# Two mixtures in 9 blocks of 512 columns instead of 10 of 464, with one load buffer for q and k and new planner settings

## The chip, the cores and the metric
The kernel runs on one core of a Trainium2 chip. The metric is the time of one execution on the device in microseconds (us), of which several runs are taken; a profile is one more execution, recorded by the hardware. TensorE does the matrix products (PE in the profile, PEld for its weight loads), VectorE (DVE), ScalarE (ACT) and GpSimd (POOL) do elementwise work, and SyncE (SP) issues all transfers, in one queue and in order.

## The reference
Three layers follow one another, all in f32, with batch 8, sequence 576 and model width 512. First an attention with 8 heads of 64 that keeps only scores close to the row's maximum:

```python
scores = scale * np.matmul(q, k.transpose(0, 1, 3, 2))
thresh = np.max(scores, axis=-1, keepdims=True) - tau
scores = np.where(scores >= thresh, scores, -1000000000.0)
attn = softmax(scores); x = np.matmul(attn, v)        # heads side by side: (8, 576, 512)
```

Then a first mixture, in which each position is mixed with the one before it in the same sequence (`mu_k * x + (1 - mu_k) * x_prev`, and the same with `mu_r`), and a second, whose gate is a convolution of 5 taps along the sequence:

```python
v = np.maximum(xk @ w_k, 0.0) ** 2 @ w_v              # 512 -> 1024 -> 512
x = sigmoid(xr @ w_r) * v
gate = sigmoid(sum(conv_w[j] * x shifted by 4 - j))   # zero before the start of a sequence
out = (gate * (x @ w_val)) @ w_out
```

## The kernel before
Activations lie transposed: 128 partitions of the model width (four of them, KD = 4) by positions. For accuracy every matmul operand of the mixtures is split in a rounded high part and a rest ("h" and "l", "hi" and "lo" in the names), and each product is the sum of three matmuls: high by high, high weights by the rest, and the weights' rest by high. `mm3` (line 719) writes this order, and all mixture matmuls are issued in line 728. The weights w_k and w_v come as 64-bit floats and are turned into the two parts on the chip by `split_weight` (line 354: two ScalarE, one VectorE and two GpSimd operations and the two that make the parts, in pieces of 512 columns; w_v's pieces go through one staging buffer, w_k's through three).

The attention goes over 32 pairs of heads, each in 9 chunks (`chunk`, line 477): QK matmuls (line 501), minimum on VectorE (526), exp on ScalarE (539), mask on VectorE (548), norm on GpSimd (561), a copy of the probabilities from p to pr by a transfer (615), transposes (585), and the AV matmuls at chunks 3 and 8 (651, 654). `prep` (418) loads q and k of one head of the next pair into a buffer "raw" (428), casts q (435) and k (431) on ScalarE, makes k's rest kl on VectorE (439) and q's rest on GpSimd (445), and frees the buffer. There are two such buffers (RAWS = 2, line 281), and the loads are planned at chunk 1 and chunk 4.

The first mixture (`moe1`, 833) works on blocks of TW = 464 columns. Each sequence is preceded by 4 columns of zeros (PAD = 4), so 8 sequences are 8 x 580 = 4640 columns, 10 blocks; the zeros let a block run over the end of a sequence without regard to it. `mix_k` (814) makes the mixed input of a block by `shift_mix` (762), in one operation per sequence that the block touches; then come 96 matmuls with w_k, a relu, a square and a split, and 96 with w_v. The results v go to memory. The second mixture (`block2`, 943) loads x and v of each block, mixes x (lines 775 and 785, over the whole block at once), makes r (48 matmuls), a sigmoid, y = gate x v (994), the convolution (tap 0 on ScalarE, 1033, taps 1 to 4 on VectorE, 1036, on a tile that has 4 columns of the block before ahead of it), then val and out (48 matmuls each), and stores.

The order of all this on each engine is written out by a planner (`Plan.order`, line 81) before the program is built: each operation has an engine, a duration, a key (lower goes first) and tokens for its buffers, and a list schedule turns them into one fixed order for each engine. At run time each engine keeps to that order and waits by semaphores. The keys hang on constants in lines 201 to 232: one unit is a batch of attention, softmax work of chunk g has the key g/36 - EARLY, and so on.

Of the kernel before, what the change touches and what calls it, by code (L numbers as in the profile page):

```python
# [40 lines left out]


# [13 lines left out]
class Plan:  # L56
# [24 lines left out]
    def order(self, hop):  # L81
# [22 lines left out]
        while events:  # L104
# [11 lines left out]
            for e in ENGINES:  # L116
                while busy[e] <= now and ready[e]:
# [73 lines left out]
                    for x in pick.after:  # L191
                        x.ready = max(x.ready, end + pick.lat + (SAME.get(e, 0.0) if x.eng == e else hop))
# [35 lines left out]
SWITCH = 200.0  # L228
GANG = 2.6953
# [8 lines left out]
def body(ctx, tc, qka, qkb, vp, w_k, w_v, w_r, w_val, w_out, conv_w, par, out):  # L238
# [14 lines left out]
    v_d = [dram.tile([128, KD, TW], F32, name=f"v_d{n}") for n in range(NBK)]  # L253
# [27 lines left out]
    XBUFS, RAWS = 6, 2  # L281
# [40 lines left out]
    SQ, K_LO = {"act": 497, "pool": 1160}, {"dve": 555, "pool": 1160}  # L322
# [396 lines left out]
    def mm3(ps, w, a, m, kcs):  # L719
# [13 lines left out]
    def product(w, a, m, K, parts, prio, rel=(), cap=("mm",), each=()):  # L733
# [7 lines left out]
        for run, uses, first, end in mm3(ps, w, a, m, list(range(K))):  # L741
# [10 lines left out]
            o = op("pe", 210 * len(uses), go, deps, prio, acq=cap + (BANKS,) if first else (),  # L752
# [9 lines left out]
    def shift_mix(w, src, prio, tiles, pool_, tag, toks, eng, opened=None, psum=False):  # L762
# [4 lines left out]
        for c in range(KD):  # L767
# [3 lines left out]
            for x, (get, at, k, deps) in enumerate(got):  # L771
                def prev(c=c, f=f, get=get, at=at, k=k, x=x):
                    if psum:
                        f["p"] = bank(f["op"])[:, 0:TW]
                        nc.scalar.activation(out=f["p"], in_=get()[:, 0:k], func=AF.Copy, scale=omu[w][:, c:c + 1])
                        return
                    if x == 0:
                        f["f"] = f["p"] = pool_().tile([128, TW], F32, name="xf", tag="xf", bufs=2)
# [3 lines left out]
                def mix(c=c, f=f, get=get, at=at, k=k):  # L782
                    if psum:
                        f["f"] = pool_().tile([128, TW], F32, name="xf", tag="xf", bufs=2)
# [4 lines left out]
                if psum:  # L789
                    o = f["op"] = chain("mix", op("act", 497, prev, first + [last.get("mix")], prio, acq=(BANKS, "xp")))  # L790
                    ps.append(chain("mixd", op("dve", 130 + 1.04 * k, mix, (o, last.get("mixd")), prio, acq=toks[:1],
                                               rel=(o, "xp"))))
                    continue
# [12 lines left out]
            h = chain(tag, op("act", 497, hi, ps + [last.get(tag), opened], prio, acq=toks[1](c)))  # L806
            l = f["lo"] = op(eng, 0, lo, (h,), prio, rel=toks[:1], port=True)
# [6 lines left out]
    def mix_k(n, prio):  # L814
        def src(c):
            return [(lambda b=b, s0=s0, k=k: x_t[b, c][:, s0:s0 + k + 1], at, k, (x_done[b, c],))
                    for b, s0, k, at in pieces(n)]

        def tiles(c):
            return [m1_p.tile([128, TW], F32R, name="xk" + x, tag="xk" + x, bufs=XKBUFS) for x in "hl"]  # L820
# [334 lines left out]
```

## Time and profile before

| | |
|---|---|
| time, median of 3 runs | 1237.56 us (1234.44 to 1240.56) |
| the profiled execution | 1239.84 us, span from the first to the last instruction 1238.1 us |
| busy in the span | PE 1200.3 us (97%), PEld 1013.0, DVE 865.2 (70%), ACT 868.8 (70%), POOL 723.3 (58%) |
| mixture matmuls (line 728) | 47% of the chain of waits that ended last |
| granted TensorE clock, mean | 0.996 |

Busy times of PE overlap, since its matmuls are pipelined and their ends are modelled; how fast they follow each other is read from their starts. Times in the rows are us from the start of the span, "ns" where it says mean.

### The profile page before, as it was taken

The numbers are of one execution on the slowest core, as the hardware profiler recorded it, in microseconds if no ns is written. First come the engines' busy times: TensorE is split into PE (matmuls) and PEld (weight loads), VectorE is DVE, ScalarE is ACT, GpSimd is POOL, SyncE is SP. The second block draws the span as 40 slices with busy tenths as digits, with TensorE's granted clock in tenths as the row PEclk, the third lists the DMA queues.
The fourth block names the chain that finished last, engine by engine and source line by source line (L and its number), as shares of the span: only waits on it lengthen the run. The fifth ranks groups of instructions, "written<-read, shape, count | busy, mean of one in ns | idle before, by whom it ended". The sixth has DMA issues, their size and how long they took to land.

```text
span 1238.1 us, 21148 instructions
## 1 busy us (share of the span) xinstructions
PE 1200.3 (97%) x7134; PEld 1013.0 (82%) x7134; DVE 865.2 (70%) x1894; ACT 868.8 (70%) x1673; POOL 723.3 (58%) x979
## 2 busy tenths in 40 slices
PE   6889999999999999999999999999999999999998
PEld 4667788877888888787878788888888888888887
DVE  7999887787788898787778687751315985555440
ACT  7899877876887886785776785763545775555442
POOL 5798866875776887466666564540306764444321
PEclk9899999999999999999999999999999999999999
DMA  6366545567456666455645455225106332221011
GB/s 241 108 198 243 204 183 208 206 205 278 175 198 245 233 209 224 166 216 188 221 157 219 156 188 191 114 114 199 62 16 238 109 123 92 93 93 62 31 46 62
DMA packets 71501, 201.62 MB, mean 163 GB/s; under 512 B 10848, under 2 KB 28384, under 8 KB 70624
## 3 DMA queue, kind: packets, MB, share of 16 engines
q1 hardware_dynamic: 71392, 200.26, 45.5%
q8 instruction: 57, 0.93, 0.3%
q14 instruction: 52, 0.43, 0.1%
HBM read 91.18 MB, written 34.73 MB: 102 GB/s over the span
## 4 chain that ended last, share of the span: by engine, by line
PE 67%; DMA 4%; ACT 3%; DVE 1%; issue 1%; POOL 1%; ACTq 0%; DVEq 0%; POOLq 0%; SPq 0%
PE g L728 47%; PE s L501 8%; PE g L651 6%; PE g L585 4%; DMA pr<-p 4%; PE g L654 2%; ACT p L539 1%; DVE p L548 1%; ACT pt L598 0%; POOL p L561 0%; DVE sm L526 0%; DVE kl L439 0%; POOL qkh L445 0%; ACT qkh L431 0%; POOL sm L529 0%
## 5 line engine op out<-in xcount | busy, mean ns | idle before, releaser
L548 DVE SCALAR_TENSOR_TENSOR p<-s,sm,p 128x576 f32<-128x576 f32 x288 | 229.3, 812 | 58.6 <-ACT p L539 43.5
L526 DVE TENSOR_REDUCE sm<-s 128x1 f32<-128x576 f32 x288 | 212.6, 750 | 71.9 <-PE s L501 65.7
L539 ACT ACTIVATE p<-s,sm 128x576 f32<-128x576 f32 x288 | 210.0, 750 | 59.7 <-DVE sm L526 31.1
L561 POOL TENSOR_SCALAR p<-p,sm 128x576 f32<-128x576 f32 x234 | 189.1, 814 | 107.3 <-DVE sm L558 96.8
L501 PE MATMUL s<-qkh 128*128 128x288 f32 x620 | 196.6, 333 | 10.5 <-DVE p L548 8.0
L501 PE MATMUL s<-kl,qkh 128*128 128x288 f32 x620 | 173.6, 295 | 0.0
L598 ACT ACTIVATE pt<-g 128x512 f32<-128x512 f32 x256 | 145.0, 606 | 22.5 <-PE g L585 21.3
L529 POOL TENSOR_SCALAR sm<-sm,gs 128x1 f32<-128x1 f32 x288 | 110.4, 386 | 79.9 <-DVE sm L526 63.7
L651 PE MATMUL g<-pt,v 128*64 128x320 f32 (+1 forms) x1024 | 140.4, 417 | 0.7 <-ACT ptl L609 0.4
L501 PEld LDWEIGHTS s<-qkh 128*128 128x128 f32 x620 | 116.9, 188 | 22.8 <-issue 7.3
L585 PE MATMUL g<-ident_r,pr 128*128 128x128 f32 (+1 forms) x1148 | 121.6, 242 | 6.4 <-DMA pr<-p 4.0
L585 PEld LDWEIGHTS g<-ident_r,pr 128*128 128x128 f32 (+1 forms) x1148 | 116.0, 140 | 14.2 <-ACT p L539 3.5
L728 PE MATMUL g<-kh,w_v_hi 128*128 128x464 f32 x320 | 122.6, 383 | 0.0
L728 PE MATMUL g<-xkh,w_k_hi 128*128 128x464 f32 x320 | 121.2, 379 | 0.0
L501 PEld LDWEIGHTS s<-kl,qkh 128*128 128x128 f32 x620 | 117.2, 189 | 4.6
L728 PE MATMUL g<-xkh,w_k_lo 128*128 128x464 f32 x320 | 119.2, 373 | 0.0
L728 PE MATMUL g<-kh,w_v_lo 128*128 128x464 f32 x320 | 119.1, 372 | 0.0
L651 PEld LDWEIGHTS g<-pt,v 128*64 128x64 f32 x1024 | 68.7, 138 | 56.2 <-issue 11.5
L445 POOL TENSOR_TENSOR qkh<-raw,qkh 64x576 fp32r<-64x576 f32 x62 | 91.9, 1482 | 24.9 <-ACT qkh L435 18.7
L1036 DVE SCALAR_TENSOR_TENSOR g<-y,cw_t,g 128x464 f32<-128x464 f32 x160 | 103.9, 697 | 1.3 <-ACT g L1033 0.6
L1068 POOL TENSOR_TENSOR gvl<-gate,gvh 128x464 fp32r<-128x464 f32 x40 | 48.2, 1206 | 71.8 <-ACT gvh L1065 67.6
L1003 POOL TENSOR_TENSOR yl<-y,yh 128x464 fp32r<-128x464 f32 x40 | 50.6, 1272 | 63.2 <-ACT yh L1000 53.9
(113 smaller groups left out, 2678.3 us busy)
## 6 DMA issues: line engine op xcount, KB each, us to landing
pr<-p SPq DMA_DIRECT2D x112, 576.0 KB, 3.5
raw<-in_qkb SPq DMA_DIRECT2D x31, 640.0 KB, 4.6
raw<-in_qka SPq DMA_DIRECT2D x31, 608.0 KB, 3.8
v<-in_vp SPq DMA_DIRECT2D x32, 320.0 KB, 3.0
x_d<-x SPq DMA_DIRECT2D x32, 290.0 KB, 4.4
v_d<-vo SPq DMA_DIRECT2D x40, 232.0 KB, 2.0
vt<-v_d SPq DMA_DIRECT2D x10, 928.0 KB, 4.6
pr<-p SPq DMA_DIRECT2D x28, 288.0 KB, 2.7
```

The source lines that it names most:

```text
L445: nc.gpsimd.tensor_tensor(out=t["hi"][lo_rows, qs], in0=t["raw"][lo_rows, qs], in1=t["hi"][lo_rows, qs].bitcast(F32), op=ALU.subtract)
L501: nc.tensor.matmul(s_t[g][:, hh, 0:NT], lhsT=q, rhs=k, start=(i == 0), stop=(i == len(terms) - 1))
L526: nc.vector.tensor_reduce(out=sm[:, 0:1], in_=s_t[g][:, :, 0:NT], op=ALU.min, axis=AX.XY)
L529: nc.gpsimd.tensor_scalar(out=sm_t[g][:, 1:2], in0=sm_t[g][:, 0:1], scalar1=tau_t, scalar2=1.0, op0=ALU.add, op1=ALU.mult)
L539: nc.scalar.activation(out=view(), in_=s_t[g][:, :, 0:NT], func=AF.Exp, bias=sm_t[g][:, 0:1], scale=-1.0)
L548: nc.vector.scalar_tensor_tensor(out=view(), in0=s_t[g][:, :, 0:NT], scalar=sm[:, 1:2], in1=view(), op0=ALU.is_le, op1=ALU.mult, accum_out=to)
L561: nc.gpsimd.tensor_scalar(out=view(), in0=view(), scalar1=sm_t[g][:, 3:4], scalar2=1.0, op0=ALU.mult, op1=ALU.mult)
L585: nc.tensor.transpose(o_.bitcast(F32R), in_=i_.bitcast(F32R), identity=ident_r)
L598: nc.scalar.activation(out=pt[:, head, :, q0:q0 + 128], in_=ps.rearrange("p (k q) -> p k q", k=4), func=AF.Copy)
L651: nc.tensor.matmul(acc[h * 64:h * 64 + 64, 0:n], lhsT=v[:, kc * 128 + h * 64:kc * 128 + h * 64 + 64], rhs=pt[:, h, kc, 0:n], start=(kc == ...
L728: nc.tensor.matmul(ps()[:, 0:TW], lhsT=W[w][wt][:, kc, m * 128:(m + 1) * 128].bitcast(F32R), rhs=a(at, kc), start=(i == 0 and x == 0), sto ...
L1036: nc.vector.scalar_tensor_tensor(out=f["ps"], in0=t["y"][:, c, k:k + TW], scalar=cw[:, c, k:k + 1], in1=f["ps"], op0=ALU.mult, op1=ALU.add)
```

## The change
Both mixtures go over 9 blocks of MW = 512 columns of the 8 x 576 = 4608 columns, without padding. A generator `spans` gives the pieces of a block that lie in one sequence; 7 of the 9 blocks have two, the first and the last have one. The first mixture had one operation per piece already in its mix; now the second mixture's x mix has one ScalarE and one VectorE operation per piece too, and each convolution tap on VectorE one per piece, cut short at a sequence's start. The tap that ScalarE does is now the one without shift, which doesn't wait for the 4 columns of the block before. x is loaded with one more column per piece. The buffers for v in the second mixture go from 2 to 1, those of its output from 3 to 2, and the load buffers of q and k from 2 to 1 (RAWS). The planner gets durations for the new width, 471 ns more latency after each transfer (DMA_MARGIN), 0.2% on the durations of three engines (MARGIN), and new values for nearly all keys. The cut diff:

```diff
+MW = 512
+NM = B * S // MW
+def spans(at, end):
+    start = at
+    while at < end:
+        b, s = divmod(at, S)
+        k = min(S - s, end - at)
+        yield b, s + PAD, k, at - start
+        at += k
 ...
+                    if e in ("dve", "act", "pool"):
+                        pick.dur *= MARGIN
 ...
-                        x.ready = max(x.ready, end + pick.lat + (SAME.get(e, 0.0) if x.eng == e else hop))
+                        x.ready = max(x.ready, end + pick.lat + (DMA_MARGIN if e == "dma" else 0.0) + (SAME.get(e, 0.0) if x.eng == e else hop))
 ...
-EARLY, QK_EARLY, T_LATE, EV_EARLY, AV_LATE = 12.6663, 0.7557, -0.5953, 253.4919, 0.4078
+EARLY, QK_EARLY, T_LATE, EV_EARLY, AV_LATE = 13.0706, 0.7631, -0.6414, 57.4969, 0.5687
-MOE_LAG = 0.4575
-MOE_STEP = 0.816
+MOE_LAG = 0.6961
+MOE_STEP = 0.8287
-MIX_EARLY, SIDE_EARLY = 0.978, 0.0233
-W_KEY, W_STEP = -3.2244, 709.0823
-V_KEY, V_STEP = 3.7242, -1.2805
+MIX_EARLY, SIDE_EARLY = -4.6463, 0.4707
+W_KEY, W_STEP = -3.234, 266.006
+V_KEY, V_STEP = 18.3214, -0.5937
-HOP = 240.0
-VAL_LAG, OUT_LAG = 1.7452, 2.9004
-LATE2, LOAD2, MIX2, CONV_LAG, THR_EARLY = -13.6721, -99.7979, 7.3987, 1044.9074, 358.4791
-MIX_AT = 28.3782
-OUT_FETCH = 281.3772
-PORT_TOL, PORT_SLACK = 1851.8404, 0.196
+HOP, DMA_MARGIN, MARGIN = 257.8425, 470.7487, 1.002
+VAL_LAG, OUT_LAG = 1.5662, 2.9644
+LATE2, LOAD2, MIX2, CONV_LAG, THR_EARLY = 6.1443, -14.9596, -12.7571, 18129.9782, 561.2799
+MIX_AT = 431.1075
+OUT_FETCH = 278.4628
+PORT_TOL, PORT_SLACK = 1556.9636, 1.1934
-GANG = 2.6953
+GANG = 6.4091
 ...
-    XBUFS, RAWS = 6, 2
+    XBUFS, RAWS = 6, 1
 ...
-                    nc.tensor.matmul(ps()[:, 0:TW], lhsT=W[w][wt][:, kc, m * 128:(m + 1) * 128].bitcast(F32R),
+                    nc.tensor.matmul(ps()[:, 0:tw], lhsT=W[w][wt][:, kc, m * 128:(m + 1) * 128].bitcast(F32R),
 ...
-    for n in range(NBK):
-        moe1(n, 1 + MOE_LAG + n * MOE_STEP)
+    for n in range(NM):
+        moe1(n, 1 + MOE_LAG + n * MOE_STEP * MW / TW)
 ...
-                  vt=2, y=2, yh=2, gv=2, o=3, cv=CVB, xp=2)
+                  vt=1, y=2, yh=2, gv=2, o=2, cv=CVB, xp=2)
 ...
             def tap(c=c, k=1, f=f):
-                nc.vector.scalar_tensor_tensor(out=f["ps"], in0=t["y"][:, c, k:k + TW],
-                                               scalar=cw[:, c, k:k + 1], in1=f["ps"],
-                                               op0=ALU.mult, op1=ALU.add)
+                for b, s0, w, at in parts_of:
+                    x = at + (4 - k if s0 == PAD else 0)
+                    nc.vector.scalar_tensor_tensor(out=f["ps"][:, x:at + w], in0=t["y"][:, c, x + k:at + w + k],
+                                                   scalar=cw[:, c, k:k + 1], in1=f["ps"][:, x:at + w],
+                                                   op0=ALU.mult, op1=ALU.add)
```

## Rows read from the trace of the kernel before
**Rows 1.** Busy time by windows: us; PE, PEld, DVE, ACT, POOL; clock, DMA, GB/s
```profile
0.00:50.00 50.00, 38.16 (x215) 25.45 (x215) 39.52 (x77) 38.56 (x74) 31.60 (x53) 0.93 0.61 209
50.00:100.00 50.00, 42.47 (x292) 31.42 (x291) 47.62 (x98) 48.90 (x99) 45.12 (x67) 1.00 0.43 142
100.00:150.00 50.00, 47.20 (x323) 39.10 (x322) 44.25 (x90) 43.84 (x88) 44.16 (x60) 1.00 0.66 234
...
950.00:1000.00 50.00, 50.00 (x241) 44.86 (x240) 47.70 (x77) 40.05 (x77) 38.60 (x34) 1.00 0.41 142
```
**Rows 2.** The chain that ended last, in order of time: start us, us, what
```profile
307.77 1.88 PE g L651 x16
...
353.34 2.30 PE g L651 x16
...
846.74 98.16 PE g L728 x467
944.91 288.94 PE g L728 x1381
```
**Rows 3.** TensorE's groups: names, shape, count, busy us, mean ns, idle before
```profile
L728 PE MATMUL g<-xkh,w_k_hi 128*128 128x464 f32 x320 | 121.2, 379 | 0.0
...
L728 PE MATMUL g<-xrh,w_r_hi 128*128 128x464 f32 x160 | 59.7, 373 | 0.0
```
**Rows 4.** TensorE's timeline: start us, us, what; QK steps, then mixture steps
```profile
310.24 0.30 PE L501 MATMUL s<-kl,qkh 128*128 128x288 f32 x1
...
311.57 0.29 PE L501 MATMUL s<-kl,qkh 128*128 128x288 f32 x1
...
1211.16 0.37 PE L728 MATMUL g<-yh,w_val_hi 128*128 128x464 f32 x1
...
1216.16 0.37 PE L728 MATMUL g<-yh,w_val_hi 128*128 128x464 f32 x1
```
**Rows 5.** VectorE's groups: taps, kl, two sizes of the first mix
```profile
L1036 DVE SCALAR_TENSOR_TENSOR g<-y,cw_t,g 128x464 f32<-128x464 f32 x160 | 103.9, 697 | 1.3 <-ACT g L1033 0.6
...
L439 DVE SCALAR_TENSOR_TENSOR kl<-raw,gs,qkh 128x640 fp32r<-128x640 f32 x31 | 44.2, 1426 | 0.6 <-ACT qkh L431 0.5
...
L785 DVE SCALAR_TENSOR_TENSOR xf<-x,par_t,xf 128x464 f32<-128x464 f32 x16 | 13.7, 858 | 1.3 <-POOL xt L958 0.8 <-POOL xf L779 0.6
...
L785 DVE SCALAR_TENSOR_TENSOR xf<-x,par_t,xf 128x116 f32<-128x116 f32 x16 | 8.8, 549 | 6.3 <-POOL xf L779 6.2
```
**Rows 6.** Waits, of TensorE and of SP's queue: us in total, times, longest us
```profile
PE g L585 <- DMA pr<-p: 4.0, 6, 1.5
...
SPq L428 <- DVE kl L439: 111.9, 35, 11.6
...
SPq L966 <- DVE y L994: 50.6, 8, 14.1
```
**Rows 7.** Two pairs' casts, loads and rests on the timeline; raw's time to land
```profile
410.40 0.76 ACT L435 ACTIVATE qkh<-raw 128x640 fp32r<-128x640 f32 x1
...
432.80 0.77 ACT L435 ACTIVATE qkh<-raw 128x640 fp32r<-128x640 f32 x1
...
435.91 0.79 ACT L435 ACTIVATE qkh<-raw 128x640 fp32r<-128x640 f32 x1
...
444.33 1.42 POOL L445 TENSOR_TENSOR qkh<-raw,qkh 64x576 fp32r<-64x576 f32 x1
...
437.58 0.33 SPq L428 DMA_DIRECT2D raw<-in_qka  x1
...
DMA to landing us min/median/max: 3.4/4.1/9.4
```
**Rows 8.** Busy time of the mixture matmuls alone in one window
```profile
200.00:250.00 50.00, 23.79 (x100) 17.86 (x100) 1.00 0.59 209
```
**Rows 9.** The rests of w_v: duration ns, first and last start us
```profile
L375 POOL TENSOR_TENSOR w_v_lo<-stage,w_v_hi x8: 1272/1285/1303, 20.1 to 153.3; 128x512 fp32r<-128x512 f32 x8
```
**Rows 10.** The last eviction on the timeline
```profile
1233.87 0.56 ACT L1084 ACTIVATE o<-g 128x464 f32<-128x464 f32 x1 [1.90 <-PE g L728]
```

More of the change, by code (lines that the diff above doesn't have):

```diff
@@ L252, in body @@
     x_d = [dram.tile([128, KD, SP], F32, name=f"x_d{b}") for b in range(B)]
-    v_d = [dram.tile([128, KD, TW], F32, name=f"v_d{n}") for n in range(NBK)]
+    v_d = [dram.tile([128, KD, MW], F32, name=f"v_d{n}") for n in range(NM)]
     par_t = const.tile([128, 160], F32, name="par_t")
@@ L731, in mm3, with product @@
             yield run, [(kc, at) for _, kc, at in piece], i == 0, i == len(pieces) - 1
-    def product(w, a, m, K, parts, prio, rel=(), cap=("mm",), each=()):
+    def product(w, a, m, K, parts, prio, rel=(), cap=("mm",), each=(), tw=TW):
         t = {}
@@ L740, in product @@
         o = None
-        for run, uses, first, end in mm3(ps, w, a, m, list(range(K))):
+        for run, uses, first, end in mm3(ps, w, a, m, list(range(K)), tw):
             def go(run=run, first=first):
@@ L789, in shift_mix @@
                 if psum:
[L790 to L792 removed]
+                    o = chain("mix", op("act", 110 + 0.834 * k, prev, first + [last.get("mix")], prio,
+                                        acq=() if x else (BANKS, "xp")))
+                    f["op"] = f.get("op", o)
+                    ps.append(chain("mixd", op("dve", 130 + 1.04 * k, mix, (o, last.get("mixd")), prio,
+                                               acq=() if x else toks[:1],
+                                               rel=(f["op"], "xp") if x == len(got) - 1 else ())))
                     continue
@@ L805, in lo @@
                     out=t[c][1], in0=f["f"], in1=t[c][0].bitcast(F32), op=ALU.subtract)
-            h = chain(tag, op("act", 497, hi, ps + [last.get(tag), opened], prio, acq=toks[1](c)))
-            l = f["lo"] = op(eng, 0, lo, (h,), prio, rel=toks[:1], port=True)
+            h = chain(tag, op("act", 497 + (tw - TW) / 1.2, hi, ps + [last.get(tag), opened], prio, acq=toks[1](c)))
+            l = f["lo"] = op({x: y + (tw - TW) * (2.2 if x == "pool" else 1.04) for x, y in eng.items()}, 0, lo, (h,), prio,
+                             rel=toks[:1], port=True)
             parts.append((h, l))
@@ L816, in src @@
             return [(lambda b=b, s0=s0, k=k: x_t[b, c][:, s0:s0 + k + 1], at, k, (x_done[b, c],))
-                    for b, s0, k, at in pieces(n)]
+                    for b, s0, k, at in spans(n * MW, n * MW + MW)]
         def tiles(c):
-            return [m1_p.tile([128, TW], F32R, name="xk" + x, tag="xk" + x, bufs=XKBUFS) for x in "hl"]
-        get, parts, ends = shift_mix("k", src, prio, tiles, lambda: m1_p, "xk", ("xf", lambda c: ("xk",)), X_LO)
+            return [m1_p.tile([128, MW], F32R, name="xk" + x, tag="xk" + x, bufs=XKBUFS) for x in "hl"]
+        get, parts, ends = shift_mix("k", src, prio, tiles, lambda: m1_p, "xk", ("xf", lambda c: ("xk",)), X_LO, tw=MW)
         xm[n] = (get, parts)
-        for x, (b, s0, k, at) in enumerate(pieces(n)):
+        for x, (b, s0, k, at) in enumerate(spans(n * MW, n * MW + MW)):
             if s0 + k == SP:
@@ L952, in tile_ @@
         def tile_(k, extra=0, dt=F32, where="b", bufs=None):
-            t[k] = pool[where].tile([128, KD, TW + extra], dt, name=k, tag=k, bufs=bufs)
+            t[k] = pool[where].tile([128, KD, MW + extra], dt, name=k, tag=k, bufs=bufs)
+        parts_of = list(spans(n * MW, n * MW + MW))
         def load_x():
-            tile_("xt", 1, where="a")
-            if n * TW % SP == 0:
-                nc.gpsimd.memset(t["xt"][:, :, 0:1], 0.0)
-            for b, s0, k, at in pieces(n):
-                if at == 0 and s0:
-                    s0, k, at = s0 - 1, k + 1, -1
-                nc.sync.dma_start(out=t["xt"][:, :, 1 + at:1 + at + k], in_=x_d[b][:, :, s0:s0 + k])
+            tile_("xt", 2, where="a")
+            for x, (b, s0, k, at) in enumerate(parts_of):
+                nc.sync.dma_start(out=t["xt"][:, :, at + x:at + x + k + 1], in_=x_d[b][:, :, s0 - 1:s0 + k])
@@ L964, in load_v @@
         def load_v():
-            tile_("vt", where="b")
+            tile_("vt", where="b", bufs=1)
             nc.sync.dma_start(out=t["vt"], in_=v_d[n])
-        lx = chain("lx", dma(2048 * TW, load_x, (free_a, last.get("lx")), se, acq=("xt",)))
-        lv = chain("lv", dma(2048 * TW, load_v, [end_1, last.get("lv")] + v_by[n], base - 1, acq=("vt",)))
+        lx = chain("lx", dma(2048 * MW, load_x, (free_a, last.get("lx")), se, acq=("xt",)))
+        lv = chain("lv", dma(2048 * MW, load_v, [end_1, last.get("lv")] + v_by[n], base - 1, acq=("vt",)))
```

112 lines of the change are left out of this document (56 added, 56 removed).

## The prediction
> **What bounds the kernel now.** First the windows of 50 us, which give each engine's busy time by stretch [rows 1]. From 950 us on TensorE is busy 50.00 of 50.00 us with every other engine below it, the nearest being VectorE at 47.70. Only the start is loose: 11.84, 7.53 and 2.80 us of TensorE are idle in the first three windows, 22.2 us together, while VectorE, ScalarE and GpSimd stand at 45 to 49 of 50 in the second of them. Then the chain of waits [rows 2]: it is TensorE in line 728, the mixtures' matmuls, 467 of them in 98.16 us and then 1381 in 288.94 us without one wait between. So after the attention (846.74 us) the time is the number of those matmuls times their spacing, and before it TensorE is what all the work passes through. The granted clock is 1.00, the 2.4 GHz level, in all the windows shown but the first (0.93). The forecast therefore rests on two things: what the matmuls cost, and whether something new keeps TensorE waiting.
>
> **The matmuls: the term that carries the sum.** Six groups of 320 (both operands of w_k and w_v) and nine of 160 (w_r, w_val, w_out) make 3360 matmuls of 464 columns [rows 3]. With 9 blocks there are 9 x 336 = 3024 of 512. The spacing is read from starts, not from durations, because the durations overlap (369 to 383 ns of one, though they follow each other faster): from 1211.16 to 1216.16 us lie 24 steps, 208.3 ns each [rows 4]; at 2.4 GHz the 464 columns alone would be 193.3 ns, so 15 ns come with each instruction. What do 48 more columns cost? Sixteen AV matmuls of 256 columns take 1.88 us and sixteen of 320 take 2.30 us [rows 2]: 26.3 ns for 64 columns, 0.41 ns each, which leaves the rest fixed: 228.3 ns at 512. Ten QK steps of 288 columns take 1.33 us, 133.0 ns each [rows 4]; from there to 464 the slope is 0.428 ns, which gives 228.9 ns. Before: 3360 x 208.3 = 700.0 us. After: 690.5 us by the first slope, 692.2 us by the second. That is -9.5 to -7.8 us; I take -8.6, between the two, since no row lies beyond 464 columns. About two fifths of it (144 of 336 per block) lies in the second mixture, where TensorE never waits, and the rest in a stretch where it nearly never does.
> The Trainium skill (TensorE: Matmul & The Clock Gate, section "Wait - 56ns, not 53.3ns?") gives a fixed cost of about 2.5 ns per matmul above the columns. By it there would be little to save in having fewer instructions: an estimate from that page is 3360 x 195.8 - 3024 x 215.8 = 5.3 us. The trace's 15 ns at 464 columns does not agree with it, and the measurement decides.
>
> **The other engines in the first mixture.** They lose a tenth of their instructions and each is a tenth longer; the fixed part falls away. They work beside TensorE, so I cost this at nothing. The cover is TensorE's own work.
>
> **The split at sequence ends.** Without the padding a block that crosses from one sequence to the next is two spans: 7 of the 9 blocks, 16 spans in all. Convolution taps and the r mixture then need one VectorE instruction per span. A tap of 464 columns takes 697 ns [rows 5]; at one column per 1.04 ns (the planner's own slope) 214 ns of that is fixed. Two spans: 512 x 1.04 + 2 x 214 = 961 ns. Per block VectorE has 16 taps and 12 other operations of this width (4 mixes, 4 y, 4 gate products), which I put at a tap's length: 28 x 0.697 = 19.5 us of the 30.0 us in which TensorE does a block (144 x 208.3 ns). After, with 20 of them split and 8 at 746 ns: 20 x 0.961 + 8 x 0.746 = 25.2 us of 32.9 (144 x 228.5 ns). The upper bound takes the fixed part from the SBUF mixes, 549 ns for 116 columns and 858 for 464 [rows 5], 446 ns fixed and 0.89 per column: 1347 ns for a split one, 902 for a whole one, and 34.2 us of 32.9, so VectorE would bind by 1.3 us in each of 7 blocks. I take the tap's own row, as most of the split operations are taps: cost nothing, bounds 0 to 9 us. The place to fear is 950 to 1000 us, where VectorE is already at 47.70; the block there first, block 0, has one span.
> One v buffer instead of two: the load of block n+1 now waits for the last y product of block n, on SP, with output stores and x loads behind it. SP stood 8 times behind y already, 50.6 us in all [rows 6], and TensorE lost nothing by it. A block lasts 32.9 us, long beside the slowest load of raw (9.4 us [rows 7]), so nothing is taken here.
>
> **One load buffer for q and k.** In the attention each pair needs two loads. The casts of one pair begin at 410.40 us and of the next at 432.80, a period of 22.4 us [rows 7]. With one buffer all of it is in series: load (4.1 us median), cast to release (432.80 to the next issue at 437.58 us: 4.8), load (4.1), cast to release of the second head (435.91 to the end of its q rest at 445.75: 9.8). That is 22.8 us if nobody hurries, against 22.4; with the q rest done at once, as for the first head, 17.8. The planner knows of the one buffer and orders the rest earlier, and its new latency of 0.47 us per transfer makes 4.1 us of load about what it now counts. I take 0 because q and k are cast a whole pair ahead of use. But the cover is thin: what the cycle exceeds the pair's period by is paid 31 times, since TensorE's order is fixed and matmuls behind a late QK don't pass it. Bounds 0 to +31 us (1 us a pair).
> The loads stand on SP's queue ahead of moves of p; already now loads of raw wait 111.9 us for kl in 35 waits, and TensorE waits 4.0 us for the moves [rows 6]. With the buffer's wait at all 60 loads, or with a plan that counts transfers right, this can go to 0 or to 12 us. I take 4 again: no change.
>
> **New keys.** Weights, mixes and side work get other priorities. At first TensorE has only attention; later 50 us hold 100 mixture matmuls beside it [rows 8], 20.8 us of work. Each us by which the mixture starts later or earlier is thus worth up to 0.42 us, less what attention gains by having TensorE to itself. The w_v split, whose last piece starts at 153.3 us [rows 9], goes from keys of about 4 down to -5 to keys of 18 down to 14, behind the q and k casts and the mixes. Its eight pieces start between 20.1 and 153.3 us, 19 us apart; two pieces late are 38 us, at most +16 us. On the early side the mixture can't begin before the first batch's attention is done, so I allow half a piece, 10 us, -4 us. I take 0, as softmax stood ahead of it already.
>
> **The end.** After the last matmul there is one eviction of 0.56 us [rows 10] and one store, both a tenth longer: +0.2 us.
>
> **Sum.** -8.6 + 0.2 = -8.4 us from the profiled execution's 1239.84 us (span 1238.1, 1.74 around it), which is 1231.4. That execution is 2.3 us above the median of the three runs, so on the median: 1237.56 - 8.4 = **1229**.
>
> **The rivals.**
> - *The keys gain too.* Of the 22.2 us of idle TensorE at the start, 16 follow after the first load; if half of that goes, 8 us more: **1221**. For it: those are waits of attention on three full engines, from which the w_v split is moved away. Against: the total of their work stays.
> - *The saving is given back on the queue of transfers.* The waits on moved p go from 4 to 12 us: **1237**. For: SP is in order and the single buffer puts a wait before each load. Against: the longer latency in the plan pulls the other way.
> - *The cost of a matmul follows its columns.* 208.3 x 512/464 = 229.9 ns, 695.2 us in all, -4.8: **1233**. The AV rows speak against it. The Trainium skill's page named above lands near this by its small fixed cost (-5.3 us, 1232).
> - *The single buffer stalls QK, the slower one.* Place: the QK matmuls of every second chunk, behind the second head's load. Price: 31 times the excess. 0.27 us a pair takes the whole gain, 0.47 make the kernel slower by 0.5%, and 0.8 us give 1237.56 - 8.4 + 24.8 = **1254**. For: 22.8 us of cycle against 22.4, and kl of the second head takes 1426 ns [rows 5] where the planner counts 801. Against: no QK matmul waits for kl now, and the q rest has only to come earlier.
> - That the change doesn't do what it says can hardly be: the block width is in every matmul.
>
> **How the numbers follow.** Forecast 0.50; keys gain 0.12; given back 0.17; cost by columns 0.06; stall 0.15. A measurement of this kernel can tell about 0.5%, 6.2 us, so the borders are 1231.4 and 1243.7. Faster: nearly nine tenths of the forecast (its own range 1224 to 1234) and the keys' gain: 0.56. Within: the rest of the forecast, given back, and cost by columns: 0.28. Slower: the stall and a worse give-back: 0.16. The range reaches over the keys' gain and the given-back case to the weak form of the stall, 1214 to 1245.
>
> **What would show it.** In the trace of after: starts of line 728's matmuls 228 to 229 ns apart in the last 200 us, 3024 of them, and no wait between the end of attention and the last one. Waits of QK on kl or on q's rest would show the stall, a longer list of waits on moved p the giving back, and TensorE's idle time up to 150 us (22.2 now) the keys. Wrong is the prediction if TensorE stands in the second mixture, or if the spacing is not near 228.6 ns.

## The result and the profile after

The changed kernel takes 1226.04 us (median of 5, 1222.22 to 1229.45) where the kernel before took 1237.56: a ratio of 0.9909, 95% interval 0.988 to 0.9937. The forecast of 1229 us had the sign and nearly the size. The terms behind it are another matter: the one that carried the sum gave less than a third of what was forecast, and the attention, for which I had forecast no change but its share of the matmuls, gave more than the whole of it.

From the page of the profile after, the span and the busy time of each engine:

```profile
span 1224.3 us, 20506 instructions
...
PE 1193.0 (97%) x6798; PEld 950.0 (78%) x6798; DVE 875.0 (71%) x1991; ACT 864.3 (71%) x1633; POOL 734.2 (60%) x971
```

The span is 13.8 us shorter than before (1238.1). The windows after, with the columns of [rows 1]:

```profile
0.00:50.00 50.00, 37.93 (x224) 25.04 (x224) 39.89 (x79) 42.48 (x83) 36.81 (x57) 1.00 0.59 200
50.00:100.00 50.00, 44.54 (x298) 33.70 (x299) 47.85 (x101) 46.71 (x93) 45.99 (x68) 0.97 0.47 153
100.00:150.00 50.00, 49.55 (x310) 39.23 (x309) 41.87 (x81) 43.43 (x84) 38.65 (x53) 0.97 0.57 200
...
950.00:1000.00 50.00, 49.80 (x216) 39.94 (x215) 48.71 (x97) 36.78 (x70) 34.55 (x27) 1.00 0.30 102
1000.00:1050.00 50.00, 48.82 (x210) 38.86 (x210) 42.40 (x94) 34.92 (x67) 27.17 (x22) 1.00 0.36 118
```

Against [rows 1], TensorE's idle time in the first 150 us fell from 22.2 to 18.0 us. And TensorE is no longer busy in every microsecond of the second mixture: 0.20 us are missing from 950 to 1000 us and 1.18 us in the next window. The chain that ended last, to be read against [rows 2], shows the same break: between two long pieces of matmuls stand short pieces of VectorE.

```profile
823.45 131.65 PE g L744 x564
...
960.34 1.39 DVE y L1015
965.13 1.26 DVE y L1015
...
1026.62 193.43 PE g L744 x840
```

The spacing of matmuls is read from starts on TensorE's timeline after, as in [rows 4]: first a stretch of w_v, then one of w_out.

```profile
900.03 0.39 PE L744 MATMUL g<-kh,w_v_lo 128*128 128x512 f32 x1
...
902.37 0.39 PE L744 MATMUL g<-kh,w_v_lo 128*128 128x512 f32 x1
...
1209.00 0.39 PE L744 MATMUL g<-gvh,w_out_hi 128*128 128x512 f32 x1
...
1211.72 0.39 PE L744 MATMUL g<-gvh,w_out_hi 128*128 128x512 f32 x1
```

Ten steps in 2.34 us are 234 ns; twelve steps in 2.72 us are 226.7 ns. So the spacing depends on the product, and the forecast of 228.6 ns lies at its low end. The table has the mean over all neighbouring starts of the same product up to 250 ns apart, in ns. In the attention some 5% of the gaps of w_k and w_v are longer, from 258 ns on before and from 286 ns on after; they are interruptions of the row and left out at both widths.

| product | before, 464 columns | after, 512 columns | step | saved, us |
|---|---|---|---|---|
| w_k | 210.0 | 233.1 | 23.0 | 0.3 |
| w_v | 209.8 | 233.2 | 23.4 | -0.1 |
| w_r | 210.5 | 233.4 | 22.9 | 0.2 |
| w_val | 208.4 | 229.0 | 20.6 | 1.1 |
| w_out | 208.4 | 229.0 | 20.5 | 1.1 |
| all | 209.6 | 232.0 | 22.4 | 2.6 |

The last column is matmuls times spacing, before less after: 960 against 864 for w_k and w_v, 480 against 432 for each of the others; the row "all" is weighted by these counts. Steps and savings are taken before rounding.

**Where 13.8 us went.** The matmuls gave 2.6 us. The stretch up to the last AV matmul, with the mixture matmuls in it taken off at their spacing (1513 before, 1321 after), went from 529.2 to 515.5 us: 13.7 us. The second mixture gave back 2.5: the time from the last AV matmul to the last of all, less its matmuls at their spacing, is 0.5 us before and 3.0 after. -2.6 - 13.7 + 2.5 = -13.8.

TensorE's and SP's waits after, as in [rows 6]:

```profile
PE s L517 <- DVE p L564: 6.8, 6, 2.0
PE g L601 <- DMA pr<-p: 4.9, 7, 1.4
PE g L744 <- ACT gate L1064: 0.8, 2, 0.6
PE g L744 <- DVE xf L803: 0.5, 1, 0.5
...
SPq L444 <- DVE kl L455: 90.1, 39, 5.6
```

No QK matmul waits for kl (one waits 0.3 us for a q rest, in a line not shown), and SP waits less for it than before (90.1 us against 111.9), with one load buffer instead of two. The groups of VectorE that [rows 5] has for before: a whole tap, the two parts of a split one, and the y products that read the v buffer (vt).

```profile
L1059 DVE SCALAR_TENSOR_TENSOR g<-y,cw_t,g 128x512 f32<-128x512 f32 x16 | 11.1, 749 | 0.0
L1059 DVE SCALAR_TENSOR_TENSOR g<-y,cw_t,g 128x448 f32<-128x448 f32 x16 | 10.9, 684 | 0.1
L1059 DVE SCALAR_TENSOR_TENSOR g<-y,cw_t,g 128x64 f32<-128x64 f32 x16 | 4.5, 282 | 0.0
...
L1015 DVE TENSOR_TENSOR y<-gate,vt 128x512 f32<-128x512 f32 x36 | 31.4, 879 | 47.7 <-ACT gate L1010 46.2 <-PE g L744 1.0 <-DMA vt<-v_d 0.5
```

A whole tap is 749 ns, a split one 684 + 282 = 966 ns, and VectorE stood 0.5 us in all for v. The landing time of raw and the rests of w_v, beside [rows 7] and [rows 9]:

```profile
DMA to landing us min/median/max: 3.7/4.6/8.1
...
L391 POOL TENSOR_TENSOR w_v_lo<-stage,w_v_hi x6: 1268/1282/1295, 25.1 to 138.3; 128x512 fp32r<-128x512 f32 x6
L391 DVE TENSOR_TENSOR w_v_lo<-stage,w_v_hi x2: 681/1076/1471, 122.4 to 155.5; 128x512 fp32r<-128x512 f32 x2
```

The first rest starts 5 us later than before and the last at 155.5 instead of 153.3 us. Their span is nearly the same; what VectorE does for the split in the first 50 us is not, as the experiments show.

### The profile page after: what moved, and what is told of

It is laid out like the page before. It is cut to its first block, busy times and chain, and to the rows that moved or that the text cites. A ratio compares the mean times of both kernels' runs of the same rounds, so it can differ in the third digit from the quotient of the medians.

```text
span 1224.3 us, 20506 instructions
## 1 busy us (share of the span) xinstructions
PE 1193.0 (97%) x6798; PEld 950.0 (78%) x6798; DVE 875.0 (71%) x1991; ACT 864.3 (71%) x1633; POOL 734.2 (60%) x971
## 4 chain that ended last, share of the span: by engine, by line
PE 77%; DVE 7%; ACT 5%; DMA 4%; POOL 4%; issue 3%; SPq 0%; POOLq 0%; DVEq 0%; ACTq 0%
PE g L744 48%; PE s L517 11%; PE g L667 8%; PE g L601 6%; DMA pr<-p 3%; DVE g L1059 3%; PE g L670 3%; ACT p L555 1%; DVE p L564 1%; DVE xf L803 1%; ACT pt L614 1%; POOL sm L545 1%; POOL p L577 1%; DVE y L1015 1%; POOL qkh L461 1%
## 5 line engine op out<-in xcount | busy, mean ns | idle before, releaser
L614 ACT ACTIVATE pt<-g 128x512 f32<-128x512 f32 x256 | 145.4, 601 | 32.7 <-PE g L601 28.9
L545 POOL TENSOR_SCALAR sm<-sm,gs 128x1 f32<-128x1 f32 x288 | 117.6, 410 | 75.7 <-DVE sm L542 52.8
L601 PEld LDWEIGHTS g<-ident_r,pr 128*128 128x128 f32 (+1 forms) x1148 | 116.6, 140 | 16.8 <-issue 3.3
L1059 DVE SCALAR_TENSOR_TENSOR g<-y,cw_t,g 128x192 f32<-128x192 f32 (+26 forms) x256 | 125.5, 517 | 4.2
L744 PE MATMUL g<-kh,w_v_hi 128*128 128x512 f32 x288 | 116.8, 406 | 0.0
L744 PE MATMUL g<-xkh,w_k_hi 128*128 128x512 f32 x288 | 116.5, 405 | 0.0
L744 PE MATMUL g<-xkh,w_k_lo 128*128 128x512 f32 x288 | 113.5, 394 | 0.0
L744 PE MATMUL g<-kh,w_v_lo 128*128 128x512 f32 x288 | 113.5, 394 | 0.0
L461 POOL TENSOR_TENSOR qkh<-raw,qkh 64x576 fp32r<-64x576 f32 x62 | 89.2, 1438 | 15.0 <-ACT qkh L451 11.1
L825 POOL TENSOR_TENSOR xrl<-xf,xrh 128x512 fp32r<-128x512 f32 x36 | 47.6, 1332 | 80.9 <-ACT xrh L822 80.5
L1024 POOL TENSOR_TENSOR yl<-y,yh 128x512 fp32r<-128x512 f32 x36 | 49.1, 1375 | 72.8 <-ACT yh L1021 72.8
```

Source lines behind the costliest of these rows:

```text
L461: nc.gpsimd.tensor_tensor(out=t["hi"][lo_rows, qs], in0=t["raw"][lo_rows, qs], in1=t["hi"][lo_rows, qs].bitcast(F32), op=ALU.subtract)
L545: nc.gpsimd.tensor_scalar(out=sm_t[g][:, 1:2], in0=sm_t[g][:, 0:1], scalar1=tau_t, scalar2=1.0, op0=ALU.add, op1=ALU.mult)
L601: nc.tensor.transpose(o_.bitcast(F32R), in_=i_.bitcast(F32R), identity=ident_r)
L614: nc.scalar.activation(out=pt[:, head, :, q0:q0 + 128], in_=ps.rearrange("p (k q) -> p k q", k=4), func=AF.Copy)
L744: nc.tensor.matmul(ps()[:, 0:tw], lhsT=W[w][wt][:, kc, m * 128:(m + 1) * 128].bitcast(F32R), rhs=a(at, kc), start=(i == 0 and x == 0), sto ...
L1059: nc.vector.scalar_tensor_tensor(out=f["ps"][:, x:at + w], in0=t["y"][:, c, x + k:at + w + k], scalar=cw[:, c, k:k + 1], in1=f["ps"][:, x: ...
```

## Experiments

Theory A: the wider blocks carry the gain, by the matmuls' spacing. Theory B: the new keys carry it, and the blocks alone bring little. Theory C, formed after the first four kernels: the single load buffer has a price, in the first batch of attention, and one pair of keys, that of the w_v split, pays it.

All numbers in one table, in us. "First mixture" is the start of the first mixture matmul; "idle" is TensorE's idle time up to the last AV matmul, with that before 150 us behind the stroke; "attention" is the time up to the last AV matmul less the mixture matmuls started by then at their spacing; "at 1.2 GHz" is the time up to the last AV matmul in which the granted clock stood at its lower level, as far as the traces record the clock. These four are worked out from one trace of each kernel. (Some expectations below have the attention column up to 2 us lower, since longer gaps went into their spacing.)

| kernel | time | ratio to before (95%) | first mixture | idle | attention | at 1.2 GHz |
|---|---|---|---|---|---|---|
| before | 1237.56 | | 109.1 | 33.5 / 22.2 | 529.2 | 10.2 |
| after | 1226.04 | 0.9909 (0.988-0.9937) | 106.5 | 25.7 / 18.0 | 515.5 | 6.8 |
| blocks_old_keys | 1263.29 | 1.0204 (1.0178-1.023) | 128.7 | 47.4 / 30.9 | 552.3 | 27.3 |
| keys_old_blocks | 1270.11 | 1.0261 (1.0235-1.0287) | 107.0 | 44.0 / 21.0 | 549.3 | 27.3 |
| raws1_only | 1259.81 | 1.018 (1.0156-1.0205) | 131.2 | 46.4 / 34.3 | 550.2 | 27.3 |
| after_no_margin | 1243.29 | 1.0045 (1.0024-1.0066) | 103.8 | 38.8 / 21.9 | 532.7 | 10.2 |
| raws1_new_vkey | 1240.46 | 1.0019 (1.0001-1.0036) | 107.5 | 31.2 / 22.1 | 529.5 | 13.7 |
| after_old_vkey | 1247.7 | 1.0073 (1.0047-1.0099) | 116.6 | 42.1 / 32.6 | 537.4 | 23.9 |
| taps_whole | 1223.71 | 0.9883 (0.9856-0.991) | 105.9 | 22.7 / 17.4 | 512.2 | 6.8 |
| raws1_vkey_margin | 1254.37 | 1.0128 (1.0107-1.0149) | 116.3 | 40.8 / 28.9 | 543.9 | 27.3 |
| blocks_vkey_margin | 1257.15 | 1.0149 (1.0124-1.0174) | 109.6 | 44.8 / 23.3 | 545.6 | 20.5 |
| after_hop | 1229.4 | 0.9923 (0.9905-0.9941) | 105.4 | 28.4 / 18.3 | 519.8 | 10.2 |

Three kernels with the same planner constants as after (after itself, taps_whole and pitch_kk below) have 515.5, 512.2 and 514.7 us in the attention column, though their edits lie elsewhere. Differences of 3 us there are not read as effects.

**Blocks and keys apart.** blocks_old_keys is the changed kernel with all planner constants of before; keys_old_blocks is the kernel before, two load buffers included, with all the new ones.

```diff
 # blocks_old_keys, from after (all constants, two shown)
-HOP, DMA_MARGIN, MARGIN = 257.8425, 470.7487, 1.002
+HOP, DMA_MARGIN, MARGIN = 240.0, 0.0, 1.0
-V_KEY, V_STEP = 18.3214, -0.5937
+V_KEY, V_STEP = 3.7242, -1.2805
```

> The changed kernel (9 blocks of 512, one load buffer) with all planner constants as they were before (old keys, no margins). Theory A (the prediction's sum: the fewer, longer matmuls carry the gain): 8 us below the kernel before or more, near 1229 us. Theory B (read from the two traces: mixture matmuls stand 209.9 ns apart before and about 232 after, so they give only some 2 to 3 us, and the order in the attention stretch gives the rest): about 1235 to 1240 us, with the time from start to the last AV matmul, less mixture matmuls at their spacing, near the 529 us of before and not the 516 of after.

> The kernel before (10 blocks of 464, two load buffers) with the new planner constants and margins. Theory A: no gain, 1235 to 1240 us or worse. Theory B: most of the gain, 1224 to 1230 us, with the attention stretch (last AV less mixture matmuls) near 516 us. A third possibility, that keys fit only the shape they were sought for: both this and the run with old keys come out above 1235 us.

Measured: 1263.29 and 1270.11 us. Each half alone loses, by 26 and 33 us. They lose in the attention column, the second half also 7 us in the second mixture, and not in the spacing (231.9 and 209.5 ns). Neither A nor B, as a sum of two independent parts, can stand. The first half still holds the single load buffer, whose own price comes next; the blocks with two load buffers and old keys were not run. The halves lose in different places. With the old keys the first mixture matmul comes 22 us late. With the new keys on the old blocks it comes in time, but the w_v rests end only at 194.4 us, and the first w_v matmul starts at 194.7 (before: 162.5). Between 150 and 200 us 12 mixture matmuls start, where it was 105 before. That window of keys_old_blocks:

```profile
150.00:200.00 50.00, 39.47 (x240) 29.95 (x238) 41.83 (x103) 37.13 (x72) 38.40 (x56) 0.83 0.52 187
```

TensorE lacks 10.5 us there, and its granted clock is 0.83.

**One load buffer, alone.** The kernel before, with nothing changed but the buffer.

```diff
-    XBUFS, RAWS = 6, 2
+    XBUFS, RAWS = 6, 1
```

> The kernel before with one load buffer for q and k instead of two, nothing else. The prediction's slow rival says the loads in series (22.8 us of cycle against a period of 22.4) make QK wait: 0.3 to 1 us for each of 31 pairs, +9 to +31 us, 1247 to 1268 us. If q and k are cast early enough: within 4 us of the kernel before, and no QK matmul waiting for kl.

Measured: 1259.81 us, 22 us slower than before. This is the price that I had set at zero, and it isn't where I looked for it. QK waits 1.7 us for kl over the whole kernel, and behind 150 us TensorE's idle time is 12.1 us, 11.3 before: the steady part pays next to nothing. The price is at the start: the loads of the first batch are issued 12.9 us apart, and its four pairs are done (start of the last copy of x on ScalarE) at 119.5 us (before: 100.5). One cycle of raws1_only on the timeline, by engine (load issues on SP, casts of q on ScalarE, rests on VectorE):

```profile
33.06 0.33 SPq L428 DMA_DIRECT2D raw<-in_qka  x1
48.51 0.33 SPq L428 DMA_DIRECT2D raw<-in_qkb  x1
...
37.51 0.73 ACT L435 ACTIVATE qkh<-raw 128x640 fp32r<-128x640 f32 x1
53.87 0.73 ACT L435 ACTIVATE qkh<-raw 128x640 fp32r<-128x640 f32 x1
...
35.42 1.76 DVE L375 TENSOR_TENSOR w_v_lo<-stage,w_v_hi 128x512 fp32r<-128x512 f32 x1
37.32 1.53 DVE L375 TENSOR_TENSOR w_k_lo<-wst,w_k_hi 128x512 fp32r<-128x512 f32 x1
...
47.56 0.92 DVE L439 SCALAR_TENSOR_TENSOR kl<-raw,gs,qkh 128x576 fp32r<-128x576 f32 x1
```

The cast of q is at 37.51 us and that of k, on which kl waits, ends at 38.90; but kl, the last reader of the buffer, runs only at 47.56, and the next load goes out 0.95 us after it starts. VectorE is busy all that time: with two weight rests until 38.85, then mostly with the softmax of earlier chunks, and another 0.81 us of the w_v split at 44.69. With two buffers it is the load after the next that waits for this kl; with one it is the next head's.

Not all of the price is waiting. The attention column grew by 21.0 us and TensorE's idle time by 12.9. The granted clock stood at 1.2 GHz for 27.3 us instead of 10.2, in three stretches before 130 us and one near 285. The third begins at 121.6 us; in the 10 us from 110 to 120 TensorE was busy for 7.17. Here is its window in raws1_only (in before the clock was 1.00 there, [rows 1]), and in it 16 AV matmuls of 256 columns, which take 1.88 us at 1.00 [rows 2]:

```profile
100.00:150.00 50.00, 43.77 (x275) 33.97 (x276) 39.31 (x78) 38.86 (x77) 30.79 (x48) 0.93 0.50 185
...
124.29 3.68 PE L651 MATMUL g<-pt,v 128*64 128x256 f32 x16
```

At the lower level they take nearly twice as long. TensorE is busy for 22.8 of the 27.3 us, before for 9.7 of the 10.2; half of the difference, 6.5 us, is my estimate of what the clock costs. Idle time and clock together are 19.4 of the 21.0 us. That the waiting brought the clock down is not shown by a run of its own.

**The w_v split's keys, alone, both ways.** To raws1_only, the new pair; to after, the old pair.

```diff
 # raws1_new_vkey, from raws1_only; after_old_vkey is the reverse, from after
-V_KEY, V_STEP = 3.7242, -1.2805
+V_KEY, V_STEP = 18.3214, -0.5937
```

> The kernel before with one load buffer (as in the run of 1260 us) and, in addition, only the new keys of the w_v split (V_KEY, V_STEP). Theory C: the single buffer costs its 22 us in the first batch, because a buffer is held until ScalarE, VectorE and GpSimd have cast it, and the w_v split of the old keys goes ahead of those casts. Then the four pairs of the first batch are done near 100 us (119.5 with the old keys, 100.5 before), loads follow each other every 10 to 11 us instead of 12 to 13, and the time is 1238 to 1245 us. Rival D: the other keys repair it; then the first batch stays near 115 to 120 us and the time at 1255 us or more.

> The changed kernel with the old keys of the w_v split alone. Theory C: the first batch is done 10 to 20 us later than the 96.3 us of the changed kernel, the first mixture matmul comes at 115 to 128 us instead of 106.5, and the time is 1236 to 1250 us. Rival D: all of this within 5 us of the changed kernel.

Measured: 1240.46 and 1247.7 us. This is the clearest result of the study. Two constants give back 19 of the 22 us that the buffer cost, and taking them out of the changed kernel costs 22 us. In raws1_new_vkey the loads are 10.0 us apart and the first batch is done at 98.6 us; in after_old_vkey it is done at 110.6 us, in after at 96.3. A cycle of raws1_new_vkey on the timeline:

```profile
34.72 0.73 ACT L435 ACTIVATE qkh<-raw 128x640 fp32r<-128x640 f32 x1
...
36.89 1.90 DVE L439 SCALAR_TENSOR_TENSOR kl<-raw,gs,qkh 128x576 fp32r<-128x576 f32 x1
...
38.85 0.33 SPq L428 DMA_DIRECT2D raw<-in_qkb  x1
```

kl starts 2.2 us after the cast of q, where it was 10.05 us in raws1_only, and the next load follows at once. What moved is the work on the split's staging buffer (stage) in the first 50 us: VectorE, ScalarE and GpSimd, first raws1_only, then raws1_new_vkey.

```profile
0.00:50.00 50.00, 6.25 (x4) 5.53 (x9) 7.63 (x7) 0.93 0.55 193
0.00:50.00 50.00, 1.35 (x2) 2.75 (x4) 3.92 (x4) 0.97 0.55 194
```

VectorE, which makes kl, does 4.9 us less of it. Between after_old_vkey and after it is 4.8 us less (7.48 and 2.69), while GpSimd there does no less of it (6.47 and 6.99). The same window of all work shows what that is worth to TensorE; the first row below is raws1_only.

```profile
0.00:50.00 50.00, 32.25 (x173) 21.34 (x174) 39.64 (x72) 38.87 (x74) 34.36 (x54) 0.93 0.55 193
```

And raws1_new_vkey:

```profile
0.00:50.00 50.00, 38.87 (x223) 26.30 (x224) 40.19 (x79) 42.15 (x81) 36.43 (x58) 0.97 0.55 194
```

after_old_vkey falls back to the first of these:

```profile
0.00:50.00 50.00, 32.26 (x178) 21.53 (x179) 39.06 (x70) 38.24 (x74) 35.05 (x56) 0.90 0.55 191
```

173 and 178 matmuls against 223 and, in after, 224. Theory C holds: the price, its place and its repair came out as it said, both ways. That VectorE is the engine that matters, among the three that theory C names, is read from the traces and was not tested by itself.

**The latency counted on transfers.** The changed kernel's plan without what it adds to durations and transfers; and, the other way, raws1_new_vkey with it.

```diff
 # after_no_margin, from after
-HOP, DMA_MARGIN, MARGIN = 257.8425, 470.7487, 1.002
+HOP, DMA_MARGIN, MARGIN = 257.8425, 0.0, 1.0
 # raws1_vkey_margin, from raws1_new_vkey, with the code of after for both
+HOP, DMA_MARGIN, MARGIN = 240.0, 470.7487, 1.002
```

> The changed kernel with the planner's two margins taken out (DMA_MARGIN 0, MARGIN 1), the other keys kept. If the margin on transfers earns its place: TensorE waits on moved p rise from 4.9 us to 8 to 15 us and the time from 1226 to 1230 to 1236 us. If it only shuffles the order: waits on moved p within 2 us of 4.9, and the time moves either way by less than 5 us.

> The kernel before with one load buffer, the new keys of the w_v split, and the two planner margins (0.47 us on transfers, 0.2% on durations); blocks of 464 and all other keys as before. If the margin by itself is worth the 17 us that its removal cost the changed kernel: 1223 to 1230 us, with the attention stretch less mixture matmuls near 515 us (527.7 without it). If the margin pays only together with keys that were sought with it: 1235 to 1255 us.

Measured: 1243.29 and 1254.37 us: taking the margins out of the changed kernel costs 17 us, more than the 4 to 10 expected, and putting them into the other one costs 14. TensorE's waits in after_no_margin:

```profile
PE g L601 <- DMA pr<-p: 12.9, 17, 2.4
PE s L517 <- DVE p L564: 10.2, 8, 2.7
```

The waits on moved p go from 4.9 to 12.9 us and those on p from 6.8 to 10.2, 11 us of the 17. So the margins, in the changed kernel, go with fewer waits on transfers, as the name says; the two were not tried apart. But they are no improvement that can be carried over by themselves: with the old values of the other constants the same two numbers lose.

**What else the keys hold.** blocks_vkey_margin is the changed kernel with old constants, but for the w_v keys and the margins. after_hop moves a single constant a little.

```diff
 # after_hop, from after
-HOP, DMA_MARGIN, MARGIN = 257.8425, 470.7487, 1.002
+HOP, DMA_MARGIN, MARGIN = 257.0, 470.7487, 1.002
```

> The changed kernel with the margins and the new keys of the w_v split, but all other keys as before. If these two are what the keys do: 1223 to 1232 us. If the other keys matter as well: 1236 us or more, against 1263 us with all old keys and no margins.

> The changed kernel with one planner constant moved by a third of a percent: HOP, the time from an operation's end to a waiting one on another engine, 257.0 ns instead of 257.8425. Nothing in the work changes. If the gain lies in what the keys mean (what goes ahead of what), within 4 us of the changed kernel, 1222 to 1230 us. If it lies in one found order among many that are worse, 1230 to 1245 us.

Measured: 1257.15 and 1229.4 us. So the w_v keys and the margins together don't carry the gain; the remaining constants are worth another 31 us with these blocks. Which of them is open. That the set is not a lucky point is shown by after_hop only for that one constant: 0.3% of it leaves the plan ahead of before, and its 3.4 us over after aren't clear of noise, as the intervals of the two ratios overlap.

**Taps as one instruction.** The changed kernel with one tap instruction for a whole block, as before.

```diff
-                for b, s0, w, at in parts_of:
-                    x = at + (4 - k if s0 == PAD else 0)
-                    nc.vector.scalar_tensor_tensor(out=f["ps"][:, x:at + w], in0=t["y"][:, c, x + k:at + w + k],
...
+                nc.vector.scalar_tensor_tensor(out=f["ps"], in0=t["y"][:, c, k:k + MW],
```

> The changed kernel with each convolution tap on VectorE as one operation over the whole block, planned as before, so that the order stays the same; at the 7 places where a sequence starts inside a block the taps then reach into the sequence before, and no tap is cut short at a sequence's start. If the split taps make VectorE hold up TensorE between 950 and 1030 us: TensorE's waits on gate and xf there (1.3 us shown) go and the time falls by 2 to 4 us, to 1222 to 1224. If VectorE has room: within 1 us.

Measured: 1223.71 us, 2.3 below after, with overlapping intervals; the time alone doesn't separate them. The trace does. The windows of taps_whole, and its one wait of a mixture matmul on the gate:

```profile
950.00:1000.00 50.00, 49.81 (x216) 40.15 (x216) 45.15 (x72) 38.02 (x74) 33.59 (x27) 1.00 0.33 115
1000.00:1050.00 50.00, 50.00 (x218) 40.68 (x217) 36.34 (x64) 36.13 (x70) 25.75 (x21) 1.00 0.28 91
...
PE g L744 <- ACT gate L1062: 0.2, 1, 0.2
```

VectorE goes from 48.71 to 45.15 us in the first of them and from 42.40 to 36.34 in the second, TensorE from 48.82 to 50.00, and the time after the last AV matmul beyond its matmuls goes from 3.0 to 1.0 us. In every trace of a kernel with split taps and whole matmuls this time is 3.0 us or more. The split costs 2 us, there.

**What a column costs.** Four widths inside one kernel, dealt out by the product's tile number (the first matmul of each accumulation stays whole), and then the wide k tiles with 8 unused columns behind each row.

```diff
 # widths, from after
+                    n = tw if i == 0 and x == 0 else (512, 496, 480, 464)[m % 4]
-                    nc.tensor.matmul(ps()[:, 0:tw], lhsT=W[w][wt][:, kc, m * 128:(m + 1) * 128].bitcast(F32R),
+                    nc.tensor.matmul(ps()[:, 0:n], lhsT=W[w][wt][:, kc, m * 128:(m + 1) * 128].bitcast(F32R),
 # pitch_kk, from after
-                kt[m] = [wk["p"].tile([128, MW], F32R, name="k" + x, tag="k" + x) for x in "hl"]
+                kt[m] = [wk["p"].tile([128, MW + 8], F32R, name="k" + x, tag="k" + x)[:, 0:MW] for x in "hl"]
```

> The changed kernel with all but the first matmul of each mixture product cut to 512, 496, 480 or 464 columns, by output part m = 0, 1, 2, 3, so that one trace has the spacing at four widths in the same tiles (columns are left out, the output is not the reference's). If a fixed cost stands on each matmul and a column costs 1/2.4 ns: 6.7 ns less per 16 columns, 211.7 ns at 464 against 231.7 at 512. If the spacing follows the columns (0.4525 ns each): 7.24 ns less per 16, 210.0 at 464.

> The changed kernel with the tiles that feed the w_v product (kh, kl) allocated 520 columns wide, of which 512 are used; w_k's operands stay. If the place of the tiles in memory makes the 2 ns by which 512-wide tiles are slower at equal width (213 ns at 464 columns in the run with four widths, 210 before): w_v's matmuls stand about 230 to 231 ns apart instead of 233, w_k's stay at 233. If not: both 233.

widths took 1200.25 us in one execution, with fewer columns to compute. The first and last of a run of neighbouring starts in it, four widths of the same product one behind the other:

```profile
903.75 0.39 PE L745 MATMUL g<-xrh,w_r_lo 128*128 128x496 f32 x1
905.10 0.39 PE L745 MATMUL g<-xrh,w_r_lo 128*128 128x496 f32 x1
906.45 0.38 PE L745 MATMUL g<-xrh,w_r_lo 128*128 128x480 f32 x1
907.76 0.38 PE L745 MATMUL g<-xrh,w_r_lo 128*128 128x480 f32 x1
909.08 0.37 PE L745 MATMUL g<-xrh,w_r_lo 128*128 128x464 f32 x1
910.34 0.38 PE L745 MATMUL g<-xrh,w_r_lo 128*128 128x464 f32 x1
911.40 0.39 PE L745 MATMUL g<-xrh,w_r_hi 128*128 128x512 f32 x1
912.56 0.40 PE L745 MATMUL g<-xrh,w_r_lo 128*128 128x512 f32 x1
```

Six steps each of the first three (225, 218, 210 ns) and five of the last (232). Over all products the means (gaps up to 250 ns) are 211.4, 216.7, 224.6 and 232.5 ns at 464, 480, 496 and 512 columns: 21.1 ns for 48 columns, 0.44 each, by product from 0.43 (w_v) to 0.46 (w_r). The forecast's rule had 20.0 to 20.6 ns, a spacing in proportion to the columns would have 21.9 (211.4 x 48/464); the run lies between them and doesn't decide. Between the kernels the step is 22.4 ns, more than either rule gives, because the same 464 columns take 1.8 ns more in widths than in before (211.4 against 209.6). Something other than the column count came with the change.

pitch_kk asks whether it is the distance of the tiles in SBUF, and answers in part. Its w_v matmuls, which read the padded tiles, go from 233.2 to 231.6 ns. Those of w_k, which read others, stay (233.1 and 233.0), and the other three products move by 0.1 ns. The whole time, 1223.97 us in one execution, is inside the spread of after. So 1.6 of the 3.1 ns by which the step of w_v exceeds the forecast's 20.3 go with how its tiles lie. For w_k and w_r nothing was tried.

## Why the prediction was right, and where it was not

**The spacing: the step that failed.** I read 208.3 ns from one stretch of w_val matmuls and gave it to all 3360. The stretch was at the low end: w_val and w_out have 208.4 ns, the other three, more than two thirds of all, 209.8 to 210.5, and my own [rows 2] show it, with 98.16/467 = 210.2 and 288.94/1381 = 209.2 ns. That alone would not have harmed a difference. What did is that those three take a step of 22.9 to 23.4 ns instead of my 20.3, while in w_val and w_out the step is 20.6 and 20.5, as forecast. 2.1 ns on average times 3024 matmuls are 6.4 us of the 8.6. Measured saving: 2.6 us, outside my bounds of 7.8 to 9.5. The bounds came from two slopes, and neither asked whether one product's spacing is that of another. (The first slope was not used as it was read, either: 0.41 ns a column gives 228.0 ns and -10.5 us; 228.3 is 208.3 + 48/2.4.) The level of each product was to be had in the trace of before, its step was not. Why three products step by more is open but for the 1.6 ns of w_v that pitch_kk moved.

**The rival "cost follows columns"** came nearer, with -4.8 us, but its reason isn't shown either: in proportion to the columns w_k would have 231.8 ns and w_val 230.0, and the trace has 233.1 and 229.0. The estimate from the Trainium skill (TensorE: Matmul & The Clock Gate, "Wait - 56ns, not 53.3ns?") of -5.3 us was also nearer than mine, again not for its reason: 2.5 ns of fixed cost would put the two spacings at 195.8 and 215.8 ns, and the trace has 209.6 and 232.0.

**One load buffer, 0: wrong as a term, right as part of a pair.** The cycle that I summed, 22.8 us against a period of 22.4, was the wrong place; kl is taken in time there. In the first batch there is no such period: loads set the pace (12.9 us apart in raws1_only, 10.0 in raws1_new_vkey), and the time between a cast and the buffer's release decides. I had the price inside the bounds (0 to +31, measured 22 with old keys) and named the place wrongly; and I did not think of the clock, which is about 6.5 us of it. The stall as I described it, QK waiting for kl in 31 pairs, did not occur.

**New keys, 0: wrong.** I argued that softmax stood ahead of the w_v split already and priced only how late w_v might come. The gain was at the other end: w_v's split no longer takes VectorE's time ahead of the first batch. In the changed kernel the w_v keys are worth 22 us, which pay for the buffer, and the first batch is done at 96.3 us instead of 100.5. Costing buffer and keys one by one at zero gave the right sum of those two by accident: they are +22 and -19 to -22.

**The gain beyond that.** Of the 13.7 us in the attention, 4.2 are idle time before 150 us (the rival "keys gain too" had 8) and 3.6 are idle time later (33.5 - 22.2 = 11.3 us before, 25.7 - 18.0 = 7.7 after). About 1.6 are the clock: TensorE is busy at 1.2 GHz for 9.7 us before and 6.4 after, and half of the difference counts. The last 4.3 are neither; with a noise of 3 us in this column I don't assign them. Which constants bring it is open, beyond the w_v keys and the margins.

**Moves of p, 4 us: right** (4.9), and the margins keep it there: without them they cost 12.9, a little over the upper bound I gave (12). The saving would then have been given back, and more: 1243 us against that rival's 1237.

**The split taps, 0 with bounds to +9: nearly right.** 961 ns forecast and 966 measured for a split tap, 746 and 749 for a whole one. The place to fear was named (950 to 1000 us) and is the right neighbourhood: VectorE stands at 48.71 there and TensorE loses most in the next window. The price is 2 us.

**One v buffer, 0: right.** VectorE waits 0.5 us for v, and no wait of TensorE is put down to it.

**The sum.** Matmuls missed by +6.0 us, taps and the rest of the second mixture by +2.5, and the attention, with keys and buffer at zero, by -13.7. The errors have opposite signs, and the median came out 3 us under the forecast. That it came out so near is luck. By the two signs that the prediction itself gave for being wrong it was wrong: the spacing is 232.0 ns and not near 228.6, and TensorE stands 1.4 us in the second mixture between 950 and 1050 us. The one more column per piece of x, the two output buffers and the new order of the taps were not tried by themselves.

## What to carry to other kernels

A buffer that is taken away can have its price where transfers set the pace, here the start, and not in the steady cycle; look there for who reads it last and what stands before that reader on its engine. Ask of a lost stretch also what the granted clock was in it. A list scheduler's constants are one set: the parts tried here (the blocks with the single buffer, the keys, the buffer, the margins on the one-buffer kernel) lose 14 to 33 us when taken without the rest, so a part's worth is to be measured by removing it from the whole as well as by adding it. When a sum rests on a spacing, read it from every group of matmuls that it is multiplied with, and leave out longer gaps by the same measure on both sides.

## What the runs showed that I had not expected

The spacing of matmuls of equal shape depends on the product: in after 229.0 ns for w_out and 233.4 for w_r, both 128x512 with a weight load each, at a granted clock of 1.00. Padding the rows of the moving tiles of w_v by 8 columns took 1.6 ns from each of its matmuls and left the other products as they were. Two priority constants of work that isn't needed until about 159 us (the first w_v product in after) decided 22 us of the start.
